# Up projections of the later token blocks as 512 columns in two PSUM banks, with a new order of all steps

## The chip, the cores and the metric

One core of a Trainium2 chip runs the kernel. The metric is the device time of one execution in microseconds (us); the number for a kernel is the median of its runs. Engines are named as in the profile: PE is TensorE (PEld its weight loads), DVE is VectorE, ACT is ScalarE, POOL is GpSimd, SP is SyncE, from which all DMAs of this kernel are issued.

## The reference, cut to what matters

Three parts follow one another; the output of one is the input of the next.

```python
# 1. recurrent attention: 2 batches, 8 heads, 768 tokens, 40 dims per head
m_new = max(f + m, i); f_s = exp(f + m - m_new); i_s = exp(i - m_new)
C = f_s * C + i_s * outer(v, k);  n = f_s * n + i_s * k
y = sigmoid(o) * (C @ q) / max(|n . q|, 1)
# 2. first layer, x = y as 1536 tokens x 320
x = ((x @ w_a) * (x @ w_b)) @ w_out        # 320 -> 1536 -> 320
# 3. second layer
h = x @ w_in; out = max(0.01 * h, h) @ w_out2   # 320 -> 2048 -> 320
```

## The kernel before

**Attention.** The 768 tokens of a batch are cut into six chunks of 128. For chunk `p` and batch `b` the decays inside the chunk come from scans on VectorE (`dsc`), the scores from PE (`smm`), their product from VectorE (`sat`). `out` sums scores times values and, from chunk 1 on, the carried state times the queries; `onm`, `og`, `nrm` and `nd` normalise and gate the result on VectorE, POOL, VectorE and ScalarE. `xmm` transposes it on PE, and `xh` (ScalarE) and `xl` (VectorE) leave it in SBUF as a rounded part and a rest, so that fp32r matmuls keep fp32 accuracy. `key`, `val`, `stm`, `ste` and `stk` carry the state to the next chunk. Chunk 0 needs the gates first: scans, exponentials, and a broadcast of the first chunk's decays by PE (`dmm`) with `sel`, which is made from the identity that `lc:0` loads.

**First layer.** A block is chunk `p` of both batches, 256 tokens. For each block and each of 12 `f` (128 of the 1536 hidden columns), `up` runs 16 matmuls: 8 passes (weights and tokens in rounded part and rest) for `w_a`, 8 for `w_b`. Their two results of 256 columns share one PSUM bank; the pool `ps_mm` has two banks. `e1` (ScalarE) copies the first result to SBUF, `em` (VectorE) multiplies it by the second, `eh` (ScalarE) rounds the product, `el` (VectorE) takes the rest. `dn` then runs three matmuls of 320 columns for each tile of 128 tokens, into accumulators in the four banks of `ps_dn`. After the last `f`, `ye` copies the accumulators to SBUF. Blocks 0 and 1 run interleaved, the other four one after another.

**Second layer.** The same with three blocks of 512 tokens and 16 `f`: `ym`, `yh`, `yl` transpose and split, `um` runs 8 matmuls of 512 columns into one bank, `v1`, `vh`, `vl` evict, `dd` runs 12 matmuls of 320 columns.

**Weights.** They arrive as 8-byte numbers. `lw` loads a tile (768 KB for an up weight, 640 KB for a down weight) into one of four raw buffers; `dh`, `dl` (ScalarE) and `dm` (VectorE) turn it into fp32, `dr` (ScalarE) rounds it, `ds` (POOL) computes the rest and so frees the raw buffer. Tiles 0 to 17 belong to the first layer, 18 to 33 to the second; the raw buffers of the latter take the place of attention's SBUF, which `ca` gives up.

**Order.** The string `ORDER` lists all steps by hand; each engine runs its own instructions in this order, and so does the DMA queue of SP. A step that waits holds up all that stands behind it on its engine. Semaphores follow from the tiles: a step that takes a buffer of a pool waits for the last reader of the buffer's former tile.

Of the kernel before, what the change touches and what calls it, by code (L numbers as in the profile page):

```python
# [14 lines left out]
AF = mybir.ActivationFunctionType  # L15
ALU = mybir.AluOpType
# [21 lines left out]
    out:0:1 dl:2 key:0:1 ds:0 dh:2 dl:4 sig:1:0 dh:4 onm:0:0 dsc:1:0:0 dm:4 dsc:1:0:1 onm:0:1 dm:2 ls:1:0 vo:1:0
    key:0:0 og:0:0 lw:3 smm:1:0 stm:0:0 nrm:0:0 dr:4 dl:3 dr:2 nd:0:0 sat:1:0:1 sat:1:0:0 og:0:1 nrm:0:1 dh:3
    nd:0:1 stm:0:1 ds:4 lf:1:1 ld:1:0 lq:1:0 lw:6 xmm:0:0 val:1:0 xh:0:0 xmm:0:1 xh:0:1 dl:6 dh:6 qry:1:0 ds:2  # L40
    ste:0:0 ste:0:1 xl:0:0 xl:0:1 up:0:0 dm:3 dr:3 e1:0:0 lw:5 up:0:1 out:1:0 ld:1:1 ls:1:1 dm:6 em:0:0
    dsc:1:1:0 e1:0:1 dr:6 eh:0:0 onm:1:0 el:0:0 em:0:1 ds:3 og:1:0 up:0:3 lw:7 lk:1:1 dl:5 e1:0:3 eh:0:1
    dsc:1:1:1 nrm:1:0 el:0:1 em:0:3 lw:8 vo:1:1 ds:6 dh:7 dh:5 nd:1:0 qry:1:1 val:1:1 eh:0:3 dm:5 up:0:2 smm:1:1
    e1:0:2 dn:0:0 up:0:4 em:0:2 sat:1:1:1 sat:1:1:0 out:1:1 dr:5 dl:7 eh:0:2 xmm:1:0 dn:0:1 el:0:3 sig:1:1 dm:7
    el:0:2 dr:7 onm:1:1 dh:8 dl:8 ds:5 og:1:1 nrm:1:1 ds:7 e1:0:4 lk:2:0 lw:9 ls:2:1 lw:10 lq:2:0 lf:2:0 dn:0:2
    xh:1:0 nd:1:1 dn:0:3 xmm:1:1 up:0:5 dh:9 xh:1:1 key:1:0 val:2:0 key:1:1 xl:1:0 dm:8 em:0:4 xl:1:1 eh:0:4
    e1:0:5 dh:10 dr:8 dl:10 lw:12 ds:8 stm:1:0 up:1:0 ste:1:0 em:0:5 el:0:4 e1:1:0 eh:0:5 up:1:1 dn:0:4 el:0:5
# [5 lines left out]
    lf:3:1 ld:2:1 stk:1:1 ds:12 ds:11 up:0:7 e1:0:6 eh:1:5 dr:13 onm:2:0 em:0:6 ste:2:0 el:1:5 eh:0:6 sig:2:0
    e1:0:7 lw:14 ls:3:0 lw:16 ds:13 og:2:0 qry:2:1 em:0:7 el:0:6 nrm:2:0 dsc:2:1:1 up:1:6 dn:1:4 up:1:7 dn:0:6
    lq:3:0 lw:15 smm:2:1 dn:1:5 eh:0:7 nd:2:0 dh:14 e1:1:6 dl:14 dl:17 el:0:7 em:1:6 e1:1:7 eh:1:6 dl:16 el:1:6
    em:1:7 dm:14 sat:2:1:0 eh:1:7 dh:17 up:0:8 dn:0:7 up:0:9 e1:0:8 dh:16 dl:15 em:0:8 el:1:7 sat:2:1:1 sig:3:0
    e1:0:9 eh:0:8 dh:15 dn:1:6 out:2:1 up:1:8 dsc:3:0:0 dm:16 em:0:9 dm:15 el:0:8 eh:0:9 dr:14 dr:16 dr:15
# [5 lines left out]
    el:0:11 e1:2:0 sig:3:1 eh:1:11 up:2:1 dn:0:11 el:1:11 dsc:3:1:0 em:2:0 e1:2:1 ye:0 eh:2:0 em:2:1 el:2:0
    val:3:0 key:3:0 stk:2:0 qry:3:0 key:3:1 qry:3:1 dn:1:11 up:2:2 out:3:0 up:2:3 eh:2:1 e1:2:2 em:2:2 dsc:4:0:0
    el:2:1 onm:3:0 e1:2:3 eh:2:2 dn:2:0 dn:2:1 up:2:4 og:3:0 nrm:3:0 el:2:2 em:2:3 smm:3:1 e1:2:4 eh:2:3 em:2:4
    sat:3:1:0 el:2:3 sat:3:1:1 up:2:5 e1:2:5 sig:4:0 eh:2:4 em:2:5 dn:2:2 out:3:1 stm:3:0 up:2:7 dn:2:3 eh:2:5
    nd:3:0 el:2:4 el:2:5 dsc:4:0:1 onm:3:1 lf:5:0 ls:4:0 e1:2:7 em:2:7 og:3:1 nrm:3:1 ste:3:0 dn:2:4 dn:2:5
    up:2:6 xmm:3:0 stm:3:1 up:2:8 eh:2:7 e1:2:6 em:2:6 el:2:7 e1:2:8 nd:3:1 xh:3:0 eh:2:6 lq:4:1 em:2:8 el:2:6
    ld:4:0 lk:5:0 lq:4:0 xl:3:0 up:2:9 up:2:11 dn:2:6 xmm:3:1 dn:2:7 eh:2:8 e1:2:9 em:2:9 ste:3:1 lf:4:1 lk:4:1
    dsc:5:0:1 dsc:4:1:1 el:2:8 key:4:0 vo:5:0 sig:4:1 xh:3:1 eh:2:9 e1:2:11 em:2:11 qry:4:0 el:2:9 up:2:10  # L70
    dn:2:8 xl:3:1 smm:4:0 up:3:0 e1:2:10 eh:2:11 em:2:10 el:2:11 stk:3:0 vo:4:0 vo:4:1 val:4:0 ye:1 e1:3:0
    eh:2:10 sat:4:0:0 sat:4:0:1 el:2:10 em:3:0 dsc:4:1:0 ld:4:1 up:3:1 dn:2:9 out:4:0 onm:4:0 stm:4:0 dn:2:10
    og:4:0 key:4:1 sig:5:0 eh:3:0 e1:3:1 el:3:0 ste:4:0 em:3:1 dn:2:11 up:3:2 dn:3:0 up:3:3 eh:3:1 e1:3:2 el:3:1
    nrm:4:0 em:3:2 smm:4:1 e1:3:3 eh:3:2 val:4:1 qry:4:1 stk:3:1 el:3:2 sat:4:1:0 em:3:3 sat:4:1:1 up:3:4
    stm:4:1 out:4:1 up:3:5 dn:3:1 e1:3:4 ld:5:1 lk:5:1 lq:5:1 lf:5:1 em:3:4 ste:4:1 eh:3:3 eh:3:4 nd:4:0 el:3:3
    dn:3:2 up:3:6 dn:3:3 ls:5:0 lq:5:0 ld:5:0 ls:5:1 e1:3:5 em:3:5 el:3:4 eh:3:5 e1:3:6 em:3:6 onm:4:1 el:3:5
    og:4:1 dn:3:4 xmm:4:0 up:3:7 up:3:8 xh:4:0 e1:3:7 eh:3:6 nrm:4:1 el:3:6 em:3:7 eh:3:7 nd:4:1 e1:3:8 em:3:8
    dn:3:5 el:3:7 up:3:9 e1:3:9 ye:2 xmm:4:1 up:3:10 dn:3:6 eh:3:8 dn:3:7 el:3:8 em:3:9 dn:3:8 up:3:11 e1:3:10
    xh:4:1 eh:3:9 dsc:5:0:0 dsc:5:1:1 el:3:9 xl:4:0 xl:4:1 em:3:10 dn:3:9 smm:5:0 qry:5:0 vo:5:1 stk:4:1 stk:4:0
    val:5:1 qry:5:1 e1:3:11 eh:3:10 up:4:0 val:5:0 sat:5:0:0 el:3:10 sat:5:0:1 dsc:5:1:0 smm:5:1 dn:3:10 e1:4:0  # L80
    em:3:11 em:4:0 eh:3:11 el:3:11 sat:5:1:0 sat:5:1:1 up:4:1 e1:4:1 eh:4:0 out:5:0 up:4:2 out:5:1 em:4:1 el:4:0
# [723 lines left out]
```

## Time and profile before

| | |
|---|---|
| median of 3 runs | 468.72 us (468.51 to 469.4) |
| the profiled execution | 471.06 us |
| its span, first to last instruction | 469.3 us |
| granted clock of PE, mean over the span | 0.975 of 2.4 GHz |
| PE busy | 452.1 us, 96% |
| DVE, ACT, POOL busy | 221.2, 213.2, 127.1 us |

The span is that of one profiled execution, which is some 0.5% slower than the median of the runs. Busy times of PE are those of overlapping matmuls; the distance between the starts of neighbours is what one costs.

### The profile page before, as it was taken

The page shows a single profiled execution, that of the slowest core. Times are in us where ns is not written, and L with a number is a line of the kernel's source. Part 1 is how long each engine was busy: PE and PEld are TensorE (multiplying, and loading weights), DVE is VectorE, ACT ScalarE, POOL GpSimd, SP SyncE. Part 2 cuts the span into 40 slices and gives each one's busy share as a digit, 9 for nine tenths or more (in the row PEclk, how much of TensorE's full clock was granted, in tenths as well). Part 3 has the DMA queues.
Part 4 walks back from the last instruction along what each step waited for, and adds up shares of the span by engine and source line. Part 5 has one row for each costly group of instructions (what it writes and reads, how often), then busy time and mean ns, then how long its engine had stood idle before and what let it go on. Part 6 is the DMA issues. An engine that isn't in the chain of part 4 may idle for free.

```text
span 469.3 us, 7968 instructions
## 1 busy us (share of the span) xinstructions
PE 452.1 (96%) x3158; PEld 426.1 (91%) x3158; DVE 221.2 (47%) x400; ACT 213.2 (45%) x429; POOL 127.1 (27%) x135
## 2 busy tenths in 40 slices
...
GB/s 240 337 240 305 251 269 116 306 165 110 121 43 0 178 1 156 68 2 1 35 235 49 165 103 176 121 109 2 0 1 56 1 0 1 0 57 1 1 0 58
DMA packets 26003, 47.86 MB, mean 102 GB/s; under 512 B 1801, under 2 KB 18765, under 8 KB 25965
## 3 DMA queue, kind: packets, MB, share of 16 engines
...
## 4 chain that ended last, share of the span: by engine, by line
PE 83%; DMA 7%; DVE 4%; POOL 2%; ACT 2%; issue 2%; SPq 0%; ACTq 0%; POOLq 0%; DVEq 0%
PE mm L560 26%; PE mm L588 19%; PE dn L619 10%; PE dn L621 10%; PE dn L620 10%; PE pa L429 3%; DMA y<-wd 2%; PE pa L382 2%; DMA y<-w 1%; DMA ddr<-wd 1%; PE pa L424 1%; DMA db<-ddr 1%; DVE y L241 1%; PE pa L455 1%; PE pa L651 1%
## 5 line engine op out<-in xcount | busy, mean ns | idle before, releaser
L560 PE MATMUL mm<-xh,wa 128*128 128x256 f32 x720 | 132.9, 287 | 6.3 <-POOL wa L256 2.2
L560 PEld LDWEIGHTS mm<-xh,wa 128*128 128x128 f32 x720 | 108.4, 192 | 8.0 <-issue 4.0
L560 PE MATMUL mm<-xl,wa 128*128 128x256 f32 x432 | 93.3, 285 | 0.0
L604 DVE TENSOR_TENSOR gl<-gg,gh 128x512 fp32r<-128x512 f32 x48 | 35.7, 754 | 106.6 <-ACT gh L599 106.6
L560 PEld LDWEIGHTS mm<-xl,wa 128*128 128x128 f32 x432 | 73.0, 193 | 0.1
L566 ACT ACTIVATE gg<-mm 128x256 f32<-128x256 f32 x72 | 27.5, 382 | 90.3 <-PE mm L560 80.9
L619 PE MATMUL dn<-wa,gh 128*128 128x320 f32 x192 | 59.6, 310 | 0.0
L621 PE MATMUL dn<-wa,gl 128*128 128x320 f32 x192 | 59.4, 309 | 0.0
L620 PE MATMUL dn<-wa,gh 128*128 128x320 f32 x192 | 59.2, 308 | 0.0
L580 DVE TENSOR_TENSOR gl<-gg,gh 128x256 fp32r<-128x256 f32 x72 | 43.1, 602 | 33.2 <-ACT gh L575 33.2
L594 ACT ACTIVATE gg<-mm 128x512 f32<-128x512 f32 x48 | 28.3, 595 | 63.4 <-PE mm L588 61.3
L571 DVE TENSOR_TENSOR gg<-gg,mm 128x256 f32<-128x256 f32 x72 | 29.7, 413 | 46.8 <-ACT gg L566 43.3
L619 PE MATMUL dn<-wd,gh 128*128 128x320 f32 x144 | 45.8, 318 | 0.0
L621 PE MATMUL dn<-wd,gl 128*128 128x320 f32 x144 | 44.5, 309 | 0.0
L620 PE MATMUL dn<-wd,gh 128*128 128x320 f32 x144 | 44.5, 309 | 0.0
L575 ACT ACTIVATE gh<-gg 128x256 fp32r<-128x256 f32 x72 | 29.6, 416 | 31.6 <-DVE gg L571 18.2
L599 ACT ACTIVATE gh<-gg 128x512 fp32r<-128x512 f32 x48 | 29.9, 629 | 23.1 <-PE dn L620 22.9
L620 PEld LDWEIGHTS dn<-wa,gh 128*128 128x128 f32 x192 | 36.1, 188 | 1.4
L619 PEld LDWEIGHTS dn<-wa,gh 128*128 128x128 f32 x192 | 36.0, 188 | 1.3
L621 PEld LDWEIGHTS dn<-wa,gl 128*128 128x128 f32 x192 | 36.0, 188 | 0.2 <-DVE gl L604 0.2
L588 PE MATMUL mm<-yh,wa 128*128 128x512 f32 x120 | 35.9, 396 | 0.0
L588 PE MATMUL mm<-yh,w 128*128 128x512 f32 x120 | 35.4, 392 | 0.0
...
## 6 DMA issues: line engine op xcount, KB each, us to landing
y<-w SPq DMA_DIRECT2D x12, 768.0 KB
raw<-w SPq DMA_DIRECT2D x8, 768.0 KB
...
```

Source lines behind the costliest of these rows:

```text
L560: pe.matmul(ps[:, ab], w[:, slot, ab, :], xs[lo][:, kt, :], start=i == 0, stop=i == 7)
L566: act.activation(out=g, in_=ps[:, 0], func=AF.Copy)
L571: dve.tensor_tensor(out=g, in0=g, in1=up_t.pop((blk, f))[:, 1], op=ALU.mult)
L575: act.activation(out=gh, in_=g_t[blk, f], func=AF.Copy)
L580: dve.tensor_tensor(out=gl, in0=g_t.pop((blk, f)), in1=raw_view(gh_t[1, blk, f]), op=ALU.subtract)
L588: pe.matmul(ps, w[:, slot, f % 2, :], xs[lo][:, kt, :], start=i == 0, stop=i == 7)
L594: act.activation(out=g, in_=ps, func=AF.Prelu, alpha=0.01)
L599: act.activation(out=gh, in_=g_t[2, blk, f], func=AF.Copy)
L604: dve.tensor_tensor(out=gl, in0=g_t.pop((2, blk, f)), in1=raw_view(gh_t[2, blk, f]), op=ALU.subtract)
L619: pe.matmul(ps, gh[:, cs], w[:, 0, :], start=f == 0, stop=False)
L620: pe.matmul(ps, gh[:, cs], w[:, 1, :], start=False, stop=False)
L621: pe.matmul(ps, gl[:, cs], w[:, 0, :], start=False, stop=f == last)
```

## The change

Blocks 0 and 1 stay as they are. From block 2 on, `up`, its evictions and `dn` take blocks 2 with 3, and 4 with 5, together: `width` is 512, the two results of a step go to two tiles of `ps_mm`, a bank each, and `dn` runs four tiles. So there are 48 up steps in place of 72 (768 matmuls in place of 1152). The token tiles hold two blocks. `ORDER` is new throughout; `up:3:*`, `up:5:*` and their evictions are gone from it. `dynamic_dma_scratch_size` is set to 4096.

```diff
@@ ORDER, its start: identity (lc:0) and first weights
-    lg:0 init spin spin spin spin spin spin spin spin spin spin spin spin spin spin spin spin lg:1 gs:0 gfa:0
-    gi:0 lc:0 gs:1 gfa:1 lw:1 gfb:0 sel gfb:1 gi:1 idr gef:0 gei:0 gfr gef:1 gdec lk:0:1 lk:0:0 ls:0:0 lw:0
-    dmm:1:1 dmm:0:0 dsc:0:0:0 gist:0 gei:1 smm:0:0 dmm:0:1 gcum dsc:0:1:1 dl:1 dh:1 sig:0:1 dl:0 dh:0 sdec
+    lg:0 init spin spin spin spin spin spin spin spin spin spin spin spin spin spin spin spin lg:1 lw:1 lc:0
+    ls:0:1 gs:0 lw:0 lk:0:1 ls:0:0 lw:2 gfa:0 gs:1 gfa:1 sel gfb:0 gfb:1 gi:0 smm:0:1 gi:1 dh:1 idr gef:1 gef:0
+    dl:1 gfr gei:0 gcum gist:0 dm:1 gei:1 gdec dmm:1:1 dr:1 dmm:1:0 dsc:0:1:0 dh:0 dl:0 dmm:0:0 dmm:0:1 sdec
...
@@ ORDER, around weight tile 11
-    dm:9 em:1:3 dr:9 lf:2:1 ld:2:0 ls:2:0 lw:11 lq:2:1 el:1:1 dsc:2:0:1 vo:2:1 ds:9 dn:1:0 up:1:2 smm:2:0 dn:1:1
-    dh:12 up:1:4 dl:11 e1:1:2 eh:1:3 dh:11 el:1:3 em:1:2 up:1:5 sat:2:0:0 stm:1:1 lw:13 dm:11 sat:2:0:1 vo:2:0
+    em:1:0 el:0:5 dh:10 dl:10 eh:1:0 e1:1:1 dr:9 sat:2:0:0 dsc:2:0:1 sat:2:0:1 el:1:0 em:1:1 lq:2:1 lw:12 lw:11
+    ld:2:0 ls:2:1 stk:1:0 key:2:0 dn:0:4 up:1:3 dn:0:5 stm:1:1 dn:1:0 eh:1:1 e1:1:3 dl:12 el:1:1 dm:10 em:1:3
+    dn:1:1 up:1:2 up:1:4 dr:10 dh:11 eh:1:3 e1:1:2 em:1:2 vo:2:0 ds:9 qry:2:0 ds:10 el:1:3 sig:2:1 e1:1:4 eh:1:2
...
@@ ORDER, before up:2:0, and block 2 with attention of chunks 4 and 5
+    sat:3:1:0 em:1:11 dn:0:11 stm:3:0 sat:3:1:1 eh:1:11 nd:3:0 out:3:1 ste:3:0 el:1:11 onm:3:1 xmm:3:0 dn:1:10
+    dn:1:11 lq:4:0 xh:3:0 ls:5:1 og:3:1 nrm:3:1 xl:3:0 nd:3:1 xmm:3:1 stk:3:0 xh:3:1 ye:0 xl:3:1 stm:3:1 up:2:0
...
+    eh:2:3 e1:2:4 sat:4:1:1 sig:5:1 em:2:4 el:2:3 up:2:5 stk:3:1 val:5:0 qry:5:0 key:4:1 val:4:1 val:5:1 qry:4:1
...
+    qry:5:1 stk:4:1 vo:5:0 sat:5:1:0 sat:5:1:1 e1:2:10 eh:2:9 out:5:1 dn:2:7 out:5:0 em:2:10 onm:5:0 onm:5:1
+    og:5:0 og:5:1 up:2:11 el:2:9 nrm:5:0 nrm:5:1 e1:2:11 nd:5:1 nd:5:0 xmm:5:1 xmm:5:0 xh:5:0 eh:2:10 xh:5:1
+    dn:2:8 em:2:11 el:2:10 xl:5:0 xl:5:1 ca lw:19 lw:20 dn:2:9 up:4:0 e1:4:0 dh:19 eh:2:11 lw:21 em:4:0 el:2:11
...
@@ x_hi, x_lo
-        cs = slice(c * T, c * T + T)
-        if p not in x_t:
-            x_t[p] = (
-                x_p.tile([128, 3, 256], F32R, tag="xh", name="xh"),
-                x_p.tile([128, 3, 256], F32R, tag="xl", name="xl"),
+        cs = slice((p % 2 * 2 + c) * T, (p % 2 * 2 + c) * T + T)
+        if p // 2 not in x_t:
+            x_t[p // 2] = (
+                x_p.tile([128, 3, 512], F32R, tag="xh", name="xh"),
+                x_p.tile([128, 3, 512], F32R, tag="xl", name="xl"),
...
@@ up_mm
+    def width(blk):
+        return 256 if blk < 2 else 512
+
     def up_mm(blk, f):
-        xs = x_t[blk]
-        ps = ps_mm.tile([128, 2, 256], F32, tag="mm", name="mm")
+        xs = x_t[blk // 2]
+        cs = slice(blk % 2 * 256, blk % 2 * 256 + width(blk))
+        if blk < 2:
+            ps = ps_mm.tile([128, 2, 256], F32, tag="mm", name="mm")
+            halves_ = ps[:, 0], ps[:, 1]
+        else:
+            halves_ = tuple(ps_mm.tile([128, 512], F32, tag="mm", name="mm") for _ in range(2))
         w = wa["u1", f]
         for ab in range(2):
             for i, (slot, lo, kt) in enumerate(UP_PASSES):
-                pe.matmul(ps[:, ab], w[:, slot, ab, :], xs[lo][:, kt, :], start=i == 0, stop=i == 7)
-        up_t[blk, f] = ps
+                pe.matmul(halves_[ab], w[:, slot, ab, :], xs[lo][:, kt, cs], start=i == 0, stop=i == 7)
+        up_t[blk, f] = halves_
...
@@ down, rows_ready, kernel
-        n = 2 if ph == 1 else 4
+        n = 2 if ph == 1 and blk < 2 else 4
...
-        for t in range(2):
+        for t in range(2 if blk < 2 else 4):
...
-    nc = bacc.Bacc("TRN2", target_bir_lowering=False, num_devices=1)
+    nc = bacc.Bacc("TRN2", target_bir_lowering=False, num_devices=1, dynamic_dma_scratch_size=4096)
```

## Rows read from the trace of the kernel before

**Rows 1.** The page, busy time of each engine, its share and instructions

```profile
PE 452.1 (96%) x3158; PEld 426.1 (91%) x3158; DVE 221.2 (47%) x400; ACT 213.2 (45%) x429; POOL 127.1 (27%) x135
```

**Rows 2.** Windows by stage: length, busy us (instructions) per engine, granted clock, DMA share, GB/s

```profile
33.70:76.00 42.30, 37.85 (x312) 36.55 (x312) 30.56 (x48) 26.10 (x50) 31.04 (x30) 1.00 0.84 261
...
80.00:198.00 118.00, 118.00 (x984) 116.60 (x983) 66.39 (x140) 41.42 (x105) 44.78 (x51) 1.00 0.38 115
...
290.00:466.00 176.00, 175.85 (x988) 158.96 (x986) 49.26 (x73) 75.92 (x136) 14.93 (x10) 1.00 0.09 28
```

**Rows 3.** Timeline of PE (start, us, line, operation): an up step, then a down step

```profile
176.50 0.64 PE L560 MATMUL mm<-xh,wa 128*128 128x256 f32 x4
...
178.42 0.31 PE L619 MATMUL dn<-wd,gh 128*128 128x320 f32 x1
...
179.30 0.64 PE L560 MATMUL mm<-xh,wa 128*128 128x256 f32 x4
```

**Rows 4.** Timeline of PE, second layer: two steps of eight 512-column matmuls and what follows

```profile
416.96 1.07 PE L588 MATMUL mm<-yh,w 128*128 128x512 f32 x4
...
418.78 0.31 PE L619 MATMUL dn<-wa,gh 128*128 128x320 f32 x1
...
329.07 1.10 PE L588 MATMUL mm<-yh,wa 128*128 128x512 f32 x4
...
330.94 1.09 PE L588 MATMUL mm<-yh,wa 128*128 128x512 f32 x4
```

**Rows 5.** Groups by shape: count, busy us, mean ns, idle before: 512-wide evictions

```profile
L604 DVE TENSOR_TENSOR gl<-gg,gh 128x512 fp32r<-128x512 f32 x48 | 35.7, 754 | 106.6 <-ACT gh L599 106.6
...
L599 ACT ACTIVATE gh<-gg 128x512 fp32r<-128x512 f32 x48 | 29.9, 629 | 23.1 <-PE dn L620 22.9
...
L594 ACT ACTIVATE gg<-mm 128x512 f32<-128x512 f32 x48 | 28.3, 595 | 63.4 <-PE mm L588 61.3 <-DVE gl L604 2.1
...
L387 DVE TENSOR_TENSOR at<-pa,pp 128x512 f32<-128x512 f32 x20 | 13.3, 684 | 4.6 <-PE pa L382 4.6
```

**Rows 6.** Timeline of the start: identity's issue, first decays, `out`, first up step

```profile
2.15 0.58 SPq L683 DMA_DIRECT2D ident_all<-consts  x1
...
8.90 0.66 PE L350 MATMUL mm<-fr,sel 64*128 64x128 f32 x4 [2.28 <-POOL fr L306]
...
19.61 7.05 PE L429 MATMUL dn<-kvo,at 128*128 128x41 f32 x32
...
33.78 0.74 PE L560 MATMUL mm<-xh,wa 128*128 128x256 f32 x4 [0.58 <-ACT xh L514]
```

**Rows 7.** The window of the first 20 us; then the page's DMA issues of weights

```profile
0.00:20.00 20.00, 13.49 (x72) 9.35 (x73) 15.62 (x24) 11.85 (x17) 6.85 (x15) 0.80 0.86 273
...
y<-w SPq DMA_DIRECT2D x12, 768.0 KB
```

**Rows 8.** Timeline of PE where it stood idle (in brackets: how long, and what ended it)

```profile
48.05 0.50 PE L560 MATMUL mm<-xh,wa 128*128 128x256 f32 x2 [1.29 <-POOL wa L256]
...
56.80 0.50 PE L560 MATMUL mm<-xh,wa 128*128 128x256 f32 x2 [0.88 <-POOL wa L256]
...
76.10 0.71 PE L560 MATMUL mm<-xh,wa 128*128 128x256 f32 x4 [1.85 <-ACT gg L566]
...
79.11 1.24 PE L455 MATMUL pa<-kvo 128*120 128x123 f32 x6
...
201.74 0.71 PE L560 MATMUL mm<-xh,wa 128*128 128x256 f32 x4 [1.70 <-DVE gg L571]
```

**Rows 9.** One line's durations (min/median/max, ns): `el`, then `em`; then POOL's and DVE's timelines

```profile
L580 DVE TENSOR_TENSOR gl<-gg,gh x72: 372/421/3214, 41.0 to 291.8; 128x256 fp32r<-128x256 f32 x72
...
L571 DVE TENSOR_TENSOR gg<-gg,mm x72: 368/415/424, 38.0 to 290.0; 128x256 f32<-128x256 f32 x72
...
196.62 2.04 POOL L467 TENSOR_TENSOR ct<-ct,mask 120x246 f32<-120x246 f32 x4
...
198.06 3.21 DVE L580 TENSOR_TENSOR gl<-gg,gh 128x256 fp32r<-128x256 f32 x1 [1.98 <-ACT gh L575]
```

More of the change, by code (lines that the diff above doesn't have):

```diff
@@ L38 @@
[L38 to L47, printed above, removed]
@@ L53 @@
[L53 to L57, printed above, removed]
@@ L63 @@
[L63 to L81, printed above, removed]
-    sig:5:1 e1:4:2 eh:4:1 onm:5:0 onm:5:1 em:4:2 el:4:1 dn:4:0 dn:3:11 up:4:4 og:5:0 og:5:1 up:4:3 nrm:5:1
@@ new lines @@
+    og:0:0 lw:6 lk:1:0 lq:1:0 ld:1:0 stm:0:0 stm:0:1 ds:4 sat:1:0:0 nrm:0:1 nrm:0:0 lf:1:1 sat:1:0:1 dl:3
+    ste:0:1 nd:0:0 ds:2 val:1:0 ste:0:0 nd:0:1 vo:1:0 xmm:0:0 xmm:0:1 xh:0:0 lk:1:1 lw:5 ls:1:1 lw:7 lq:1:1
+    ld:1:1 xh:0:1 xl:0:0 xl:0:1 up:0:1 up:0:0 dm:3 dl:6 dh:6 qry:1:0 dr:3 e1:0:1 e1:0:0 dm:6 em:0:1 em:0:0
+    sig:1:0 eh:0:0 eh:0:1 out:1:0 ds:3 el:0:1 onm:1:0 el:0:0 dsc:1:1:1 up:0:3 dr:6 dh:5 sig:1:1 dl:5 val:1:1
+    og:1:0 ds:6 vo:1:1 qry:1:1 dm:5 up:0:2 lw:8 e1:0:3 nrm:1:0 em:0:3 dsc:1:1:0 e1:0:2 dn:0:0 smm:1:1 dh:7 dl:7
@@ new lines @@
+    ste:2:0 el:0:6 e1:1:6 eh:0:7 dl:13 ds:12 ds:11 val:2:1 og:2:0 up:1:7 dn:0:6 dn:1:5 el:0:7 em:1:6 nrm:2:0
+    dm:13 smm:2:1 qry:2:1 stk:1:1 lw:14 lw:16 lf:3:1 up:0:8 dl:15 e1:1:7 eh:1:6 dr:13 sat:2:1:0 dl:14 dh:14
+    el:1:6 stk:2:0 ds:13 dl:16 nd:2:0 em:1:7 sat:2:1:1 eh:1:7 dh:15 e1:0:8 dsc:3:1:0 dn:1:6 out:2:1 dn:0:7
+    up:0:9 em:0:8 el:1:7 dm:14 dn:1:7 dm:15 stm:2:1 onm:2:1 dsc:3:1:1 dr:14 up:1:8 e1:0:9 eh:0:8 dr:15 og:2:1
+    val:3:1 ds:14 em:0:9 ste:2:1 nrm:2:1 nd:2:1 dh:16 eh:0:9 el:0:8 e1:1:8 xmm:2:1 xmm:2:0 up:1:9 dn:0:8 el:0:9
@@ new lines @@
+    ld:3:1 lk:3:0 lw:17 em:1:8 ds:15 vo:3:0 lq:3:0 ls:3:1 lk:4:0 lf:4:0 lq:3:1 dm:16 eh:1:8 e1:1:9 xh:2:0 xh:2:1
+    xl:2:0 em:1:9 dsc:3:0:0 eh:1:9 ld:3:0 dr:16 sig:3:0 xl:2:1 stk:2:1 ds:16 vo:3:1 el:1:8 dn:0:9 up:0:10
+    up:1:10 val:4:0 val:3:0 qry:3:0 dn:1:8 smm:3:0 e1:0:10 dl:17 sig:3:1 dh:17 el:1:9 em:0:10 e1:1:10 eh:0:10
+    sat:3:0:0 el:0:10 sat:3:0:1 dm:17 dr:17 dn:1:9 up:0:11 key:3:1 em:1:10 out:3:0 eh:1:10 e1:0:11 el:1:10
+    onm:3:0 em:0:11 up:1:11 eh:0:11 e1:1:11 og:3:0 ds:17 key:3:0 vo:4:0 qry:3:1 nrm:3:0 smm:3:1 el:0:11 dn:0:10
```

109 lines of the change are left out of this document (55 added, 54 removed).

## The prediction

> **What bounds the kernel now.** I read the page's busy shares first, then the stages in the view of windows, then TensorE's timeline row by row. The shares [rows 1] already name the engine: PE is busy for 452.1 of 469.3 us, VectorE and ScalarE for less than half. The stages [rows 2] say where it is not full. From 80 to 198 us and from 290 to 466 us PE is busy all the time at a granted clock of 1.00, which is 2.4 GHz; from the first up projection at 33.8 us to 76 us it is busy for 37.85 of 42.3 us, and that is the stretch in which weights are still being loaded and decoded. So the end is set by three things: when PE starts its projections, how many microseconds of matmuls it then has, and how long it stands still in between. The other engines count only where PE waits for them.
>
> The busy time of a matmul must not be taken for its price: neighbours overlap, so the page's mean for one is longer. The price is the distance between starts, and it is read from the timeline: an up step of 16 matmuls of 256 columns starts at 176.50 and the work behind it at 178.42, which is 1.92 us or 120 ns each [rows 3]. Of that, 256 columns at 2.4 GHz are 106.7 ns; some 13 ns come on top for each instruction.
>
> **The change part by part.** *Wider matmuls.* The change takes 24 pairs of up steps (12 f for blocks 2 with 3, 12 for 4 with 5), each pair 32 matmuls of 256 columns, and makes each a step of 16 matmuls of 512. The pair costs 2 x 1.92 = 3.84 us. A 512-column matmul of the same form runs in the second layer already: eight take 1.82 us in one place and 1.87 us in another [rows 4], so 16 cost 3.64 to 3.74 us. Looking through the second layer, the short time comes where weights and tokens lie in pools on the same side of SBUF (`w` with the first `yh`, `wa` with the second), the long one where they lie on different sides. In the first layer `wa` and `xh` are both on the left, so I take the short one. Saved: 24 x (3.84 - 3.64) = 4.8 us; with the long one 24 x 0.10 = 2.4 us. I put down 4.7. The down matmuls keep their number: four tiles per step instead of two, half as many steps.
>
> *Evictions.* 24 pairs of 256-wide steps on ScalarE and VectorE become 24 of 512. The rows for 512 are 595 and 629 ns for the two copies, 754 ns for the subtraction, and 684 ns for a VectorE product with one operand in PSUM, which I take for the multiplication [rows 5]. This is less than two narrow ones each time, and both engines have room [rows 1]: worth nothing by itself, as PE does not wait for either in steady state. What it costs if that fails is a rival below.
>
> *Two banks per step.* The pool has two banks. Before, a step filled one bank, the next step the other. Now a step fills both, so the first half of the next step needs the first copy done, its second half needs the multiplication done. The copy (0.60 us) starts when the first half ends and has the 1.82 us of the second half to hide in. The multiplication (0.7 us) starts when the second half ends and has the 1.82 us of the next first half, plus any down step of 1.76 us that lies between. The slack is about 1 us at its tightest, so I cost this at nothing, with up to 0.4 us a step if VectorE comes late.
>
> *New order, start.* The identity, loaded third before [rows 6], now comes behind a weight tile of 768 KB. At the 273 GB/s of the first 20 us [rows 7] that is 2.8 us. `sel` needs it, and the first-chunk gate step `gfb:0` now stands behind `sel` on VectorE; on ScalarE `gfr` now stands behind the long `gef:1` and a decode. I make the first decay matmuls 3 to 4 us later than 8.90 us [rows 6]. What follows takes most of that up: VectorE's five cumulative scans (2.1 us) move ahead of the decay scans into this wait, and the first `out` waits for three scans, two products and two merges (6 to 7 us), where before it started 10.7 us after the decay matmuls. I get 20.2 us for it against 19.61, and from there to the first up step the same PE work, so 0.5 us later than 33.78; bounds from the same rows, 1.5 us earlier (all of it taken up, and the 0.5 us waits of the transposes gone) to 3.5 us later (none of it).
>
> *New order, the idle places of PE.* Before, after 33.8 us, the larger ones are 1.29 and 0.88 us (rests of weights on POOL late), 1.85 us (an eviction behind a weight load that took 10 us), 1.70 us (VectorE held up), and after the third the clock is at 1.2 GHz, so that one up step takes 3.01 us instead of 1.92 [rows 8]. Together 5.7 + 1.1 = 6.8 us. In the new order each of these steps stands elsewhere. On the sync queue, weight tile 11 is issued ahead of three loads of chunk 2 that it stood behind (`lf:2:1`, `ld:2:0`, an `ls`), and eight PE steps lie between its load and its decode instead of five, some 3 us more: enough for a landing that came 1.85 us too late. POOL's rest of tile 6 has, by my count, its inputs and POOL 2 us before PE gets there. So these places probably go, but an order with some 800 steps has others: I let 2.0 of the 6.8 us come back somewhere, with bounds 0 and 9.
>
> *New order, two hand-overs.* The 512-wide steps need tokens of both blocks, so attention of chunk 3 must be wholly done before `up:2:0`, and chunk 5 before `up:4:0`. Before, half as much had to be ready each time. Behind `out:3:1` PE has only one transpose step and two down steps of 0.88 us [rows 3], about 2.1 us, while normalising, gating and copying (0.5 + 0.9 + 0.5 + 0.25 us by their groups, and some 0.6 us of hand-offs) take 2.7 us: 0.6 us idle, more if VectorE is behind. Behind `out:5:0` a whole up step (3.64 us) covers two such chains of about 4.2 us. Together I take 1.2 us, bounds 0.5 and 3.
>
> *Loads and memory.* All DMAs stay on the sync queue. Attention loads of chunks 2 and 3 now share the time with weights 9 to 17, but the stage is 180 us long and those loads are some 24 MB, 133 GB/s against the 261 GB/s that the stage from 33.7 us moved [rows 2]. The token tiles grow by 12 KB per partition, which the smaller scratch of 4096 gives back; the page's queue list shows hardware queues and instruction fetches only, so nothing used that scratch: no cost.
>
> **Sum.** The profiled execution took 471.06 us, 1.76 of them around the span, and the median of the three runs is 468.72, 2.34 below it. 471.06 - 4.7 - 6.8 + (2.0 + 1.2 + 0.5) = 463.3 us for the profiled one; less the same 2.3 this makes 461.0 us.
>
> **Rivals.** (a) *The order wins nothing.* What goes at the four idle places comes back at others; the pitch gain alone is left, with the hand-overs and the start inside what comes back: 468.7 - 4.7 = 464.0 us. For it speaks that the idle places come from loads and POOL, which have as much to do as before.
>
> (b) *The wide matmuls save little.* If they run at the long time of [rows 4], 2.4 us go; with nothing from the order, 466.3 us. A page of the Trainium skill speaks for a small gain: "TensorE: Matmul & The Clock Gate", section "Wait — 56ns, not 53.3ns?", has a fixed cost of about 2.5 ns for each warm matmul. By that, 384 matmuls fewer are 1.0 us, and the time would be 467.8. The trace has 13 ns at 256 columns, so by the row the rule understates what goes here.
>
> (c) *The other side: VectorE frees the second bank late.* `em`, which frees it, stands on VectorE behind `el` of the step before. `el` reads two operands in SBUF and can be held up: its median is 421 ns, its longest 3214, and that one ran at 198.06 while POOL was in back-to-back work from 196.62; PE's 1.70 us of idle came of it [rows 9]. The Trainium skill says why, in "SBUF — State Buffer", "Who interferes with whom": a VectorE instruction with two SBUF inputs and a GpSimd one that reads SBUF exclude each other. The trace agrees in that the multiplication, one input of which is in PSUM, has no such long cases. Now the wide `el` is longer, POOL has a run of seven instructions in block 2 (about 6.7 us by their groups), and the bank has only some 1 us of slack. This decides if PE loses more than 0.32 us in each of the 24 steps (7.7 / 24); at 0.4 us, 461.0 + 9.6 = 470.6 us. Against it: VectorE is 47% busy [rows 1], and one run of seven instructions is worth at most 4 us, once.
>
> (d) *The late start stays late.* The decay matmuls' 3.5 us reach the first up step and the idle places stay: 468.7 - 4.7 + 3.5 = 467.5 us.
>
> **How the numbers follow.** Forecast 0.60, (a) 0.17, (b) 0.07, (c) 0.10, (d) 0.06. The forecast's own range is 456.5 (1.5 us earlier start, nothing of the 6.8 back, 0.5 us hand-overs: 457; a little less if small idle places go too) to 465. For 8 in 10 I reach over (a), (b) and (d): 455.5 to 468. A measurement tells 0.2% or 0.9 us, so "same" is 467.8 to 469.7: parts of (b) and (d), 0.08. Slower: (c) with a bit of (d), 0.12. Faster: 0.80.
>
> **What the profile would show.** 768 up matmuls, half of them 512 wide, 16 of those in 3.64 us between starts (3.74: rival b). The first up step at 34.3 us (over 36: rival d). PE idle after that about 3 us in all, none over 1.5 us, the clock at 1.00 throughout. In blocks 2 and 4, waits of PE for `em`: under 1 us in all; several of 0.4 us are rival (c). Before `up:2:0` and `up:4:0` a wait for the token copies of 0.3 to 1 us each. I am wrong if the idle time of PE after 34 us is 7 us or more, or if the wide step takes 3.8 us.

## The result and the profile after

The changed kernel takes **457.44 us** (median of 4 runs, 455.65 to 459.37) against 469.06 us before (4 runs, 468.51 to 470.12): a ratio of 0.975, 95% interval 0.9705 to 0.9796. The forecast was 461.0 us, with a range from 455.5 to 468.0. The profiled execution took 455.65 us, 15.4 less than the one of before. That is 3.8 us more than the medians differ by, from one execution to the next: the profiled one of before lies 2.0 us above its median, the one here is the fastest of its four.

The page's busy shares, the granted clock in 40 slices, and the chain that ended last:

```profile
PE 446.4 (98%) x2774; PEld 404.5 (89%) x2774; DVE 209.3 (46%) x352; ACT 208.2 (46%) x381; POOL 125.5 (28%) x135
...
PEclk9569999999999999999999999999999999999999
...
PE 96%; DMA 1%; DVE 1%; ACT 1%; SPq 0%; issue 0%; POOL 0%; ACTq 0%
```

PE has 384 matmuls fewer than in [rows 1], as the change says, and its share of the span has gone from 96% to 98%. The chain that ended last is PE's own work and almost nothing else (before, PE had 83% of it, DMA 7%). The windows show where PE is full:

```profile
0.00:31.30 31.30, 27.17 (x136) 21.54 (x136) 24.50 (x46) 19.48 (x30) 15.87 (x24) 0.67 0.93 294
31.30:76.00 44.70, 44.68 (x375) 43.98 (x376) 36.91 (x61) 29.62 (x56) 30.22 (x31) 1.00 0.92 271
76.00:200.00 124.00, 124.00 (x877) 113.57 (x877) 69.98 (x133) 41.73 (x88) 49.21 (x58) 1.00 0.35 103
```

In the stretch up to 76 us, where PE had been busy for 37.85 of 42.3 us [rows 2], it is now busy for 44.68 of 44.70. The list of PE's waits holds five, in all 4.2 us, and all of them lie at or before the first up step:

```profile
PE dn L372 <- DMA stk<-stk: 1.9, 1, 1.9
PE dn L328 <- DVE wd L688: 1.0, 1, 1.0
PE mm L559 <- ACT xh L504: 0.6, 1, 0.6
PE pa L340 <- DVE pp L350: 0.5, 1, 0.5
PE mm L340 <- POOL fr L296: 0.2, 1, 0.2
```

So all places of [rows 8] are gone, and no new one has come. The timeline of PE at two wide steps (the first four matmuls of a step, those of its second half, and those of the next step):

```profile
204.86 1.09 PE L559 MATMUL mm<-xh,wa 128*128 128x512 f32 x4
206.69 1.07 PE L559 MATMUL mm<-xh,wa 128*128 128x512 f32 x4
208.51 1.07 PE L559 MATMUL mm<-xh,wa 128*128 128x512 f32 x4
```

A step of 16 takes 208.51 - 204.86 = 3.65 us, the short time of [rows 4]; two narrow steps took 3.84 [rows 3]. Last the start, PE's timeline again: the first decay matmuls, the scores, `out`, and the first up step:

```profile
11.16 1.11 PE L340 MATMUL mm<-fr,sel 64*128 64x128 f32 x4 [0.19 <-POOL fr L296]
...
16.11 2.08 PE L372 MATMUL dn<-stk 40*128 40x128 f32 x16
18.12 7.05 PE L419 MATMUL dn<-kvo,at 128*128 128x41 f32 x32
...
31.32 0.74 PE L559 MATMUL mm<-xh,wa 128*128 128x256 f32 x4 [0.60 <-ACT xh L504]
```

Against [rows 6] the decay matmuls are 2.26 us later, and yet `out` starts 1.49 us earlier and the first up step 2.46 us earlier.

The 15.4 us of the two profiled executions divide at two points. Up to the first up step: 33.78 - 31.32 = 2.5. From there to the last matmul: before 465.54 - 33.78 = 431.8, after 450.20 - 31.32 = 418.9, so 12.9, of which 24 x 0.20 = 4.8 are the wide steps (run 1) and the remaining 8.1 are put down to idle places and slow clock: before, PE stands idle for 6.2 us behind its first up step, and from 76.7 to 80.2 us its granted clock is at half, which costs 1.7; here there is neither. Next to nothing is left for what lies around (0.1).

### The profile page after: what moved, and what is told of

It is laid out like the page before. It is cut to its first block, busy times and chain, and to the rows that moved or that the text cites. A ratio compares the mean times of both kernels' runs of the same rounds, so it can differ in the third digit from the quotient of the medians.

```text
span 453.9 us, 7049 instructions
## 1 busy us (share of the span) xinstructions
PE 446.4 (98%) x2774; PEld 404.5 (89%) x2774; DVE 209.3 (46%) x352; ACT 208.2 (46%) x381; POOL 125.5 (28%) x135
## 4 chain that ended last, share of the span: by engine, by line
PE 96%; DMA 1%; DVE 1%; ACT 1%; SPq 0%; issue 0%; POOL 0%; ACTq 0%
PE mm L559 30%; PE mm L586 20%; PE dn L617 11%; PE dn L619 11%; PE dn L618 11%; PE pa L419 4%; PE pa L372 3%; PE pa L414 2%; PE dn L419 2%; PE pa L445 1%; DMA ident_all<-consts 1%; PE pa L490 1%; PE pa L649 1%; PE mm L445 1%; PE dn L372 0%; PE pa L340 0%
## 5 line engine op out<-in xcount | busy, mean ns | idle before, releaser
L559 PE MATMUL mm<-xh,wa 128*128 128x256 f32 (+1 forms) x480 | 114.8, 340 | 0.6 <-ACT xh L504 0.6
L559 PEld LDWEIGHTS mm<-xh,wa 128*128 128x128 f32 x480 | 79.8, 189 | 9.6 <-ACT xh L504 0.8
L602 DVE TENSOR_TENSOR gl<-gg,gh 128x512 fp32r<-128x512 f32 x48 | 34.2, 730 | 99.4 <-ACT gh L597 95.3
L559 PE MATMUL mm<-xl,wa 128*128 128x256 f32 (+1 forms) x288 | 79.3, 337 | 0.0
L559 PEld LDWEIGHTS mm<-xl,wa 128*128 128x128 f32 x288 | 51.1, 189 | 6.0
L564 ACT ACTIVATE gg<-mm 128x256 f32<-128x256 f32 (+1 forms) x48 | 23.4, 487 | 67.0 <-PE mm L559 51.1
L569 DVE TENSOR_TENSOR gg<-gg,mm 128x256 f32<-128x256 f32 (+1 forms) x48 | 26.2, 546 | 59.4 <-PE mm L559 35.3
L578 DVE TENSOR_TENSOR gl<-gg,gh 128x256 fp32r<-128x256 f32 (+1 forms) x48 | 36.0, 753 | 11.7 <-ACT gh L573 11.6
L573 ACT ACTIVATE gh<-gg 128x256 fp32r<-128x256 f32 (+1 forms) x48 | 25.0, 522 | 32.4 <-DVE gg L569 25.4
```

What stands on the lines that cost most here:

```text
L559: pe.matmul(halves_[ab], w[:, slot, ab, :], xs[lo][:, kt, cs], start=i == 0, stop=i == 7)
L569: dve.tensor_tensor(out=g, in0=g, in1=up_t.pop((blk, f))[1], op=ALU.mult)
L573: act.activation(out=gh, in_=g_t[blk, f], func=AF.Copy)
L578: dve.tensor_tensor(out=gl, in0=g_t.pop((blk, f)), in1=raw_view(gh_t[1, blk, f]), op=ALU.subtract)
L602: dve.tensor_tensor(out=gl, in0=g_t.pop((2, blk, f)), in1=raw_view(gh_t[2, blk, f]), op=ALU.subtract)
```

## The experiments

The theory (A in the expectations): width, start and the order behind the start each pay their part, and the parts add up. Medians of before in the batches were 468.85, 469.24 and 468.25 us.

**1. The width alone undone.** All of the new order, but each wide step issued as two groups of 256 columns into the halves of its banks.

```diff
-            for i, (slot, lo, kt) in enumerate(UP_PASSES):
-                pe.matmul(halves_[ab], w[:, slot, ab, :], xs[lo][:, kt, cs], start=i == 0, stop=i == 7)
+            for c0 in range(0, width(blk), 256):
+                xc = slice(cs.start + c0, cs.start + c0 + 256)
+                for i, (slot, lo, kt) in enumerate(UP_PASSES):
+                    pe.matmul(halves_[ab][:, c0:c0 + 256], w[:, slot, ab, :], xs[lo][:, kt, xc], start=i == 0, stop=i == 7)
```

> The changed kernel, but each wide up step issues its passes as two groups of 256 columns into the two halves of its bank; order, banks, evictions and down steps stay wide. Theory A (the width of the matmuls is worth 24 x (3.84 - 3.64) us): 4.8 us longer than the changed kernel, a step takes 3.84 us between starts, PE idle as little as there. Rival B (the whole gain is the order's, the width only trades matmuls for the same time): within 1 us of the changed kernel. Rival C (PE has slack in blocks 2 and 4 that hides it): a step takes 3.84 us but the sum grows by under 2 us.

Measured: 460.98 us (460.46 to 462.19), ratio 0.9828 (0.98 to 0.9856). In PE's timeline, the step and what stands behind it:

```profile
160.31 0.64 PE L561 MATMUL mm<-xh,wa 128*128 128x256 f32 x4
...
164.16 0.49 PE L490 MATMUL pa<-ident_all,ya 128*128 128x128 f32 x3
```

32 narrow matmuls take 3.85 us, 120.3 ns each, against 228 ns for a wide one. That is 0.20 us a step and 4.8 us in 24. The spans differ by 458.8 - 453.9 = 4.9, of which 0.57 is a later first up step, which leaves 4.3; the medians differ by 3.5 from the first measurement of the changed kernel and by 5.4 from the second (run 5). The pitch lies between these, so A holds, not B or C.

**2. The new start alone.** The kernel before, with the new order up to the first up step and the rest in its old order.

```diff
-    lg:0 init spin spin spin spin spin spin spin spin spin spin spin spin spin spin spin spin lg:1 gs:0 gfa:0
+    lg:0 init spin spin spin spin spin spin spin spin spin spin spin spin spin spin spin spin lg:1 lw:1 lc:0 ls:0:1
...
```

> The kernel before, narrow, with the new order's steps up to its first up step, then all steps that are left in the order of before. Theory A (the start is worth its 2.5 us by itself): the first up step at about 31.3 us in place of 33.8, and 2.5 us less than before in all. Rival B (weights are the bound behind the start): the first up step comes earlier, but PE's waits for the rests of tiles 6 and 7 (1.29 and 0.88 us) grow by what was won, and the sum stays within 1 us of before.

Measured: 465.75 us (464.4 to 466.95), ratio 0.9915 (0.9876 to 0.9954). From PE's timeline:

```profile
31.92 1.22 PE L557 MATMUL mm<-xh,wa 128*128 128x256 f32 x4 [0.58 <-ACT xh L511]
...
54.33 0.50 PE L557 MATMUL mm<-xh,wa 128*128 128x256 f32 x2 [0.24 <-POOL wa L253]
...
74.42 0.74 PE L557 MATMUL mm<-xh,wa 128*128 128x256 f32 x4 [0.67 <-DVE gg L568]
```

The first up step comes 1.9 us earlier. Of the idle places in the old order behind it, the one at 48.05 is gone, those at 56.80 and 76.10 [rows 8] are down to 0.24 and 0.67 us; the 1.70 us ended by `em` has stayed. So the new start cures part of what I had put down to the order behind it. Its earlier loads are the likely reason (weight tile 6 is issued at 22.56 in place of 25.74 us, tile 7 at 31.94 in place of 37.29); no run moves them alone.

**3. The old start.** The reverse: the changed kernel with the old order up to its first up step.

```diff
-    lg:0 init spin spin spin spin spin spin spin spin spin spin spin spin spin spin spin spin lg:1 lw:1 lc:0
+    lg:0 init spin spin spin spin spin spin spin spin spin spin spin spin spin spin spin spin lg:1 gs:0 gfa:0 gi:0
...
```

> The changed kernel with the order of before up to its first up step, then all steps that are left in the new order. Theory A: 2.5 us more than the changed kernel, no idle PE behind the start. Rival B (the idle places at 48 and 57 us came from the start's loads and decodes): these waits return as well, 4 to 5 us more than the changed kernel.

Measured: 460.13 us (458.73 to 461.36), ratio 0.9804 (0.9774 to 0.9835). The first up step starts at 35.02, and after it PE's list of waits is empty. So the new order behind the start needs no new start in order to be free of waits, and the start is worth 2.7 us against the first median of the changed kernel, 4.5 against the second (run 5). In the profiled executions 3.7 us are the later first up step; another 1.7 go behind it, where the granted clock is at half until 39.2 us here and until 30.3 in the changed kernel.

**4. One move alone.** The prediction had explained the 1.85 us at 76.10 by weight tile 11, which stood behind three loads. Here only that load is moved ahead of them in the kernel before.

```diff
-    dm:9 em:1:3 dr:9 lf:2:1 ld:2:0 ls:2:0 lw:11 lq:2:1 el:1:1 dsc:2:0:1 vo:2:1 ds:9 dn:1:0 up:1:2 smm:2:0 dn:1:1
+    ds:10 e1:1:3 eh:1:1 dl:12 dm:9 em:1:3 dr:9 lw:11 lf:2:1 ld:2:0 ls:2:0 lq:2:1 el:1:1 dsc:2:0:1 vo:2:1 ds:9 dn:1:0
```

> The kernel before with one step moved: weight tile 11 is loaded ahead of lf:2:1, ld:2:0 and ls:2:0. Theory A (that wait is one late load and nothing else): the idle 1.85 us at 76 us goes, the clock stays at 1.00 there, 2.9 us less than before. Rival B (the queue is full, so what is moved back is late in its place): another wait of 1 to 3 us appears within 15 us, and the sum stays within 1 us of before.

Measured: 471.21 us (469.87 to 475.58), ratio 1.0054 (1.0029 to 1.008): half a per cent slower. In PE's timeline the wait at 76 is gone, and this one has come:

```profile
71.42 1.91 PE L379 MATMUL pa<-stk 40*128 40x128 f32 x16 [2.17 <-DMA stk<-stk]
73.27 0.63 PE L616 MATMUL dn<-wd,gh 128*128 128x320 f32 x1
```

The scores of chunk 2 now wait for the load that the tile was moved ahead of, and behind these 2.17 us of idle the granted clock is at half again (a down matmul takes 0.63 us where it took 0.31 [rows 3]). The cause named for the wait was right: ScalarE's decode of tile 11 waits no more. Its rows, in the kernel before and then here:

```profile
72.61 0.79 ACT L237 ACTIVATE y<-y 128x640 int32<-128x640 uint32 x1 [3.50 <-DMA y<-wd]
```

```profile
68.60 0.78 ACT L234 ACTIVATE y<-y 128x640 int32<-128x640 uint32 x1
```

That this one move makes the kernel faster was not right. On this queue, which was full, the load that went ahead made another one late.

**5. The changed kernel once more**, with no edit, beside the next three on one chip.

> The changed kernel once more, as the measure for the kernels beside it. Theory A (its runs differ only by when PE's granted clock goes from 1.2 to 2.4 GHz, between 30 and 39 us in the profiles so far): 456 to 460 us, and after the clock has risen the same PE time as in its first profile, within 0.5 us. Rival B (the first profile was a lucky one in other places too): idle PE of 1 us or more behind the start.

Measured: 455.6 us (455.13 to 461.48, 6 runs), ratio 0.9727 (0.9689 to 0.9764). The median is a little below A's 456 to 460. Its trace again has no wait of PE behind the first up step, and from there to the last matmul it takes 449.67 - 30.72 = 418.95 us, where the first profile took 418.88. So A holds there and B does not.

**6. The identity first.** The prediction made the start late for two reasons, the identity behind a weight tile and `gfr`'s later place on ScalarE. Here the identity's load goes ahead.

```diff
-    lg:0 init spin spin spin spin spin spin spin spin spin spin spin spin spin spin spin spin lg:1 lw:1 lc:0
+    lg:0 init spin spin spin spin spin spin spin spin spin spin spin spin spin spin spin spin lc:0 lg:1 lw:1 ls:0:1
```

> The changed kernel with the identity loaded ahead of weight tile 1, as before the change. Theory A (in the new order the start is bound by PE at its low clock and by VectorE from the decay scans on, so that an earlier identity moves all of it): decay matmuls at about 9 us, first up step 1.5 to 2.5 us earlier, as much less in all. Rival B (the start is bound by loads, the values of the second batch and the scores): decay matmuls earlier, out at 18 us as now, within 0.7 us of the changed kernel.

Measured: 457.36 us (456.76 to 458.5), ratio 0.9745 (0.9726 to 0.9765). From the timeline of all engines:

```profile
6.29 0.14 DVE L688 TENSOR_TENSOR sel<-ident_all 64x16 fp32r<-64x16 f32 x1
...
10.96 0.45 POOL L292 TENSOR_TENSOR fr<-wd,fr 32x128 fp32r<-32x128 f32 x1 [2.94 <-ACT fr L291]
...
11.61 0.70 PE L337 MATMUL mm<-fr,sel 64*128 64x128 f32 x4 [0.24 <-POOL fr L293]
```

`sel` starts 1.1 us earlier than in the changed kernel (7.35 us there) and the decay matmuls come at 11.61 all the same, 0.45 us later: they wait for `fr`, GpSimd's split of the gates, and that for `gfr` on ScalarE. ScalarE's rows, in the changed kernel and then here:

```profile
7.03 0.90 ACT L223 ACTIVATE y<-y 128x768 f32<-128x768 f32 x1 [5.00 <-DMA y<-w]
...
10.14 0.29 ACT L294 ACTIVATE fr<-wd 64x128 fp32r<-64x128 f32 x1
```

```profile
7.64 0.90 ACT L220 ACTIVATE y<-y 128x768 f32<-128x768 f32 x1 [5.62 <-DMA y<-w]
...
10.59 0.29 ACT L291 ACTIVATE fr<-wd 64x128 fp32r<-64x128 f32 x1
```

ScalarE stands idle until weight tile 1 is there, and `gfr` comes behind that tile's decode, `idr`, two exponentials and a second decode. The edit is not clean: the identity now goes ahead of the second load of gates too, whose scan starts at 4.83 us in place of 4.26. Still, an identity that is there earlier does not bring the decay matmuls forward, and neither theory of this run had named the true wait.

**7. Tokens on the other side of SBUF.**

```diff
-    x_p = left.enter_context(tc.tile_pool(name="x", bufs=2, side="left"))
+    x_p = ctx.enter_context(tc.tile_pool(name="x", bufs=2, side="right"))
```

> The changed kernel with the pool of the token tiles xh and xl on the right side of SBUF, the weights staying on the left. Theory A (a 512-column matmul is dearer where weights and tokens lie on different sides, as in the second layer): a wide step takes 3.74 us between starts in place of 3.64, 2.4 us more in all; narrow steps as they were or up to 0.05 us more. Rival B (the two prices in the second layer have another cause): wide steps stay at 3.64 us, no change.

Measured: 458.12 us (457.95 to 459.4), ratio 0.9767 (0.9748 to 0.9785), 2.5 us over run 5. PE's timeline at a wide step:

```profile
206.21 1.10 PE L559 MATMUL mm<-xh,wa 128*128 128x512 f32 x4
...
209.95 1.10 PE L559 MATMUL mm<-xh,wa 128*128 128x512 f32 x4
```

3.74 us for 16 in place of 3.65, the long time of [rows 4]. 24 x 0.09 = 2.2 us, and from the first up step to the last matmul the two traces differ by 421.0 - 418.9 = 2.1. This was the one choice in the pitch term, and the place of the tokens decides it.

**8. PE kept dense in the start.** More matmuls on a tile of zeros between the start's small ones, six of them among the first `spin`s; 43 in all, where the expectation counts 20; nothing else is changed.

```diff
+    def spin_late():
+        pe.matmul(ps_att("mm"), warm, warm.unsqueeze(1).to_broadcast([128, 4, 128]))
...
-        "init": set_up, "spin": spin, "sel": make_sel, "idr": make_idr,
+        "init": set_up, "spin": spin, "sp": spin_late, "sel": make_sel, "idr": make_idr,
```

> The changed kernel with 20 more matmuls of 512 columns on zeros in the start, behind the scores, outs and state matmuls of chunk 0 and the scores of chunk 1. Theory A (the low clock from 10 to 31 us comes from the few columns that PE works on there; out and the state matmuls, 7.0 and 2.6 us at 1.2 GHz, would take half): clock 1.00 for most of 18 to 31 us, first up step 1 to 4 us earlier and always at 2.4 GHz, 2 to 5 us less in all. Rival B (VectorE's scans and products bound the start): the clock rises but the first up step stays within 1 us. Rival C (the added matmuls are in the way and the clock stays low): 20 x 0.43 us, up to 8 us more.

Measured: four runs took 456.48 to 457.02 us at a mean granted clock of 1.00; two took 469.36 and 470.11 at 0.971 and 0.967, have no trace and are left out of the ratio, and why they are so much longer stays open. Median 456.86 us, that of the four alone 456.65, ratio 0.973 (0.9714 to 0.9747). In the trace the granted clock is at 1.00 throughout, and 16 matmuls of `out` take 1.87 us where 32 took 7.05. Still the first up step comes at 32.34:

```profile
19.58 1.87 PE L421 MATMUL dn<-kvo,at 128*128 128x41 f32 x16
...
30.22 0.82 PE L330 MATMUL mm<-gg 128*128 128x512 bf16 x2 [1.22 <-DVE ct L467]
```

The row at 30.22 is one of the added matmuls, which waits for a bank that VectorE still reads, so part of the 32.34 is the addition's own doing. But VectorE's rows have not moved forward with the faster PE: its product `ya`, which the transposes need, starts at 28.22 us, and at 27.92 in the changed kernel, whose transposes start at 29.51. So a fast PE could win little here, as VectorE's own chain sets the time from which the transposes can run. That is B, at its bound: the first up step came 1.0 us later.

**9. The order behind the start, alone.** Runs 1 and 3 together: narrow groups and the old start.

> The order behind the first up step alone: the old order up to the first up step, each wide step issued as two groups of 256 columns. Theory A (the three parts of the gain add up): before it stood 469; the two runs that left out one part each (460.98 without the width, 460.13 without the new start, against 457.4 for the whole) put the start at 2.7 and the width at 3.5, so what is left is 469.06 - 457.44 - 2.7 - 3.5 = 5.4, and the time 463.6 (462.5 to 465); TensorE idles nowhere behind the start for more than 0.5 us. Rival B (the order needs the start or the width to be worth anything: with the first up step back at 35.0 and narrow groups, loads come late again): 466 or more, with a wait of over 1 us behind 45 us.

Measured: 463.66 us (462.57 to 464.75), ratio 0.9886 (0.9845 to 0.9927); no wait of PE behind the first up step at 34.24. The expected 463.6 came from adding up the parts, so they add up, to within 1 us. Against the first measurement of the changed kernel 4.6 here, 2.7 for the start (run 3) and 3.5 for the width (run 1) make 10.8, and the whole is 11.6; against the second, 4.6, 4.5 and 5.4 make 14.5, and the whole is 13.6.

**10 and 11. GpSimd made busy.** Additions of 128x320 on GpSimd in each of the 12 steps of blocks 4 and 5, started with `el`: four a step, then eight.

```diff
+    def pool_run(blk, f, n):
+        gh = raw_view(gh_t[1, blk, f][:, 0:320])
+        for i in range(n):
+            pool.tensor_tensor(out=junk[:, 1], in0=gh if i == 0 else junk[:, 0], in1=junk[:, 0], op=ALU.add)
...
-    up:4:1 dn:2:10 dn:2:11 dh:20 eh:4:0 dl:19 dl:20 e1:4:1 dm:20 el:4:0 em:4:1 dm:19 eh:4:1 dr:19 up:4:2 e1:4:2
+    dl:20 e1:4:1 dm:20 pr:4:0:8 el:4:0 em:4:1 dm:19 eh:4:1 dr:19 up:4:2 e1:4:2 dh:21 dr:20 ye:2 dl:21 ds:19 ds:20
```

> The changed kernel with four more GpSimd additions of 128x320 (about 0.75 us each, 3 us in a row) in each of the 12 steps of blocks 4 and 5, the first of them started by the same eviction (eh) that starts VectorE's subtraction (el). They price rival (c) of the prediction: VectorE held by GpSimd, the second bank free late. Theory A (VectorE can be held for a whole run of GpSimd, as the 3.21 us row of before says, but a step has more slack than that): el takes 2 to 4 us in these steps, the mean of em stays below 1 us, TensorE waits for VectorE for less than 1 us in all, and the time is that of the changed kernel (456 to 458.5). Rival B (the slack is 1 us or less): 12 steps with 2 us of wait each, 475 to 485. Rival C (GpSimd holds VectorE for no more than the end of one instruction): el below 1.6 us, the time the same.

> The same with eight additions a step (6 us in a row, 12 steps, 72 us of the 84 us of the stage). Theory A: now the run lasts into the next step, whose multiplication (em) frees the second bank; with steps 7 us apart and up:4:f+1 in need of that bank some 3 us behind the first one's end, VectorE held for 6 us shows as waits of TensorE for em of 1 to 3 us a step, 465 to 490. Rival B (em, which reads one operand from PSUM, is not held): el 4 us or more, em below 1 us, TensorE without waits for em, 456 to 460 unless the layer 2 weights that GpSimd decodes come late, which would show as waits for weight tiles instead.

Measured: 460.98 us (460.69 to 464.0), ratio 0.9852 (0.981 to 0.9893) with four; 492.99 us (492.55 to 493.98), ratio 1.0523 (1.0491 to 1.0555) with eight. VectorE was hardly held. `el` of blocks 4 and 5 (min/median/max, ns), in the changed kernel, with four and with eight:

```profile
L578 DVE TENSOR_TENSOR gl<-gg,gh x13: 678/690/1393, 209.4 to 276.7; 128x512 fp32r<-128x512 f32 x13
```

```profile
L586 DVE TENSOR_TENSOR gl<-gg,gh x13: 683/1119/1205, 211.2 to 285.1; 128x512 fp32r<-128x512 f32 x13
...
L567 DVE TENSOR_TENSOR gg<-gg,mm x48: 370/548/691, 36.1 to 280.0; 128x256 f32<-128x256 f32 x24, 128x512 f32<-128x512 f32 x24
```

```profile
L586 DVE TENSOR_TENSOR gl<-gg,gh x12: 682/921/1210, 209.6 to 287.9; 128x512 fp32r<-128x512 f32 x12
```

The median of `el` gains 0.2 to 0.4 us, the longest `el` is 1.21 us, and none takes the 3 or 6 us of the additions; the longest `em` (second line of the run with four) is 691 ns, against 689 without them. The Trainium skill, "SBUF — State Buffer", section "Who interferes with whom", lets the loser of the shared port wait for the whole of the other's instruction, and exempts a VectorE instruction with only one input in SBUF; both agree with these rows, as one addition took 0.84 to 0.88 us on average and `el` waited for 0.52 us at most.

This does not settle the 3.21 us of [rows 9], which came back: the profiles of runs 2 and 4, which have the old order in this place, show the same `el` with the same length, and PE's wait of 1.70 us behind it. GpSimd's rows in the kernel before, beside the `el` of 198.06, then that `el` in run 2 and in run 4:

```profile
198.62 0.72 POOL L402 TENSOR_TENSOR kvo<-kvo,istn 128x320 f32<-128x320 f32 x1
199.30 1.01 POOL L369 TENSOR_TENSOR q<-q,db 120x384 f32<-120x384 f32 x1
200.27 0.72 POOL L402 TENSOR_TENSOR kvo<-kvo,istn 128x320 f32<-128x320 f32 x1
```

```profile
192.31 3.21 DVE L577 TENSOR_TENSOR gl<-gg,gh 128x256 fp32r<-128x256 f32 x1 [1.98 <-ACT gh L572]
```

```profile
198.80 3.21 DVE L577 TENSOR_TENSOR gl<-gg,gh 128x256 fp32r<-128x256 f32 x1 [1.98 <-ACT gh L572]
```

`el` ends at 201.27, 0.28 us after the last of these, so it was held for the whole run of GpSimd. Each of these instructions starts some 0.04 us before the end of the one ahead of it; each addition of runs 10 and 11 starts 0.08 us after it. Whether this gap is what lets VectorE in is not shown; the additions are in any case no copy of the run that held it.

The time went another way. With eight, PE stands still for 11.90 us at 256.60, behind a copy of ScalarE. The timeline ahead of it, all engines:

```profile
239.35 7.03 POOL L582 TENSOR_TENSOR junk<-junk 128x320 f32<-128x320 f32 x7
...
247.26 1.29 POOL L244 TENSOR_TENSOR w<-raw,w 128x512 fp32r<-128x512 f32 x1
...
248.58 0.33 SPq L206 DMA_DIRECT2D raw<-wd  x1
...
252.53 0.78 ACT L221 ACTIVATE raw<-raw 128x640 f32<-128x640 f32 x1 [15.95 <-DMA raw<-wd]
...
255.97 0.57 ACT L562 ACTIVATE gg<-mm 128x512 f32<-128x512 f32 x1
```

GpSimd computes the rest of a weight tile late, so the raw buffer comes free late (248.55), the next load is issued at 248.58 and is there at 252.53; ScalarE, in order, waits 15.95 us in the decoding of that tile, and `e1` stands behind it. Behind its first up step PE stands idle for 27.7 us in all; the second long wait, 11.10 us at 314.93 in the second layer, has the same cause, a load issued at 309.36 behind GpSimd's rests:

```profile
313.50 0.90 ACT L225 ACTIVATE raw<-raw 128x768 int32<-128x768 uint32 x1 [10.98 <-DMA raw<-w]
```

With four additions PE loses 1.90 us at 248.19 in the same way and 2.09 at 270.89, at the first projection of the second layer, whose cause stays open. Of the expectations with four, C was right on VectorE and wrong on the time, A and B were wrong. With eight, A was wrong; B was right that `em` is not held and that late weights are what can cost time, and wrong on `el`.

## Why the prediction was right, point by point

**Pitch: right.** 4.7 us put down, 4.8 shown by run 1. The choice of the short time was right, for the reason given: run 7 moves the tokens and gets the long one. The rule weighed as rival (b), "TensorE: Matmul & The Clock Gate", section "Wait — 56ns, not 53.3ns?" of the Trainium skill, does not hold for these matmuls: over the columns at 2.4 GHz they cost 13.6 ns at 256 (run 1) and 14.8 ns at 512 (the step of 3.65 us), not 2.5.

**Start: the step that failed.** The forecast was 0.5 us later; it came 2.5 earlier, outside my bounds (1.5 earlier). Two errors. I made the decay matmuls 3 to 4 us later, for the identity and for `gfr`'s place on ScalarE; they came 2.26 later, and run 6 shows that it was ScalarE, behind weight tile 1, and not the identity. And I had `out` wait for three scans and two products. Its first heads need only the first half of their product: it started at 18.12, when the scores were issued and before VectorE's second product (18.27). The rest of the gain (13.20 us from `out` to the first up step, before 14.17) is at the transposes: PE waits there no longer for VectorE (before 0.39 us), and they take 1.21 us in place of 1.61. In medians the start is worth 2.7 us (run 3; 4.5 against run 5) to 3.1 (run 2).

**Idle places: right in kind, mis-sized in what comes back.** 6.8 us go; I let 2.0 come back, and nothing did. The cause given for the third place (tile 11 behind three loads) is shown by run 4, which also shows that this move by itself would not have paid. The 1.70 us of the fourth hangs on the 3.21 us `el` each time that they occur (before, runs 2 and 4). Run 2 adds what I had not seen: the new start alone removes 3.1 of the 5.7 us, so the idle places hang on both parts; the order behind the start removes all of them by itself (run 3).

**Hand-overs: mis-sized.** 1.2 us were put down, 0 measured: no wait of PE stands before `up:2:0` or `up:4:0`. PE's rows from the transposes of chunk 3 (each batch) over the state matmuls `stm:3:1` to `up:2:0`:

```profile
122.53 0.53 PE L490 MATMUL pa<-ident_all,ya 128*128 128x128 f32 x3
...
124.81 0.53 PE L490 MATMUL pa<-ident_all,ya 128*128 128x128 f32 x3
125.19 0.83 PE L445 MATMUL pa<-kvo 128*120 128x123 f32 x6
125.92 1.19 PE L559 MATMUL mm<-xh,wa 128*128 128x512 f32 x4
```

PE's own steps cover 2.28 us, about as counted (2.1), but the chain of normalising and gating, for which I had put down 2.7, is done by then; the copy behind the second transposes is covered by the state matmuls, which I had not counted.

**Two banks and evictions: right** at nothing. No wait for `em` is in PE's list. Memory was put at nothing too; no run tests it alone.

**Rivals.** (a) and (d) are refuted by the windows and by runs 3 and 9, (b) by run 1. (c), the slower side, does not happen here: the longest `el` in the profile after takes 1.54 us, and `em` is not held even by six microseconds of GpSimd in a row (run 11). But what it feared is real: the 3.21 us `el` of [rows 9] came in all three profiles with the old order in its place and in none with the new one, and runs 10 and 11, with gaps between their additions, do not price such a run of GpSimd. What decided the time there is the ring of raw weight buffers.

**Sum.** 463.3 was forecast for the profiled execution, 455.65 came: 3.0 from the start, 2.0 from what did not come back, 1.2 from the hand-overs, together 6.2 of the 7.65. Most of the rest is in smaller idle places and low clock that I had not summed: 0.43 us at 70.09, and six state matmuls that took 1.02 us in place of 0.53 behind the third place. All three errors are costs that I set too high. Two more things on the numbers: the terms named for the lower end of the forecast's own range add up to 456.2 us, not 457; and the second measurement of the changed kernel, 455.6 (run 5), lies only just inside the wider range that begins at 455.5.
